# Gate fills three steps ahead of the value fills in place of two (induced-set attention and a gated feed-forward layer)

## The chip, the core and the metric

The kernel runs on one core of one Trainium2 chip. A core has TensorE (PE, matrix products, with its weight loads shown apart as PEld), VectorE (DVE), ScalarE (ACT), GpSimd (POOL) and SyncE (SP, which here only issues DMAs). Each engine takes its instructions in the order in which the program gives them. The metric is the device time of one execution in microseconds. Three runs of the kernel before took 770.77 us at the median (770.39 to 770.82).

## The reference

The input x has 4 batches of 12416 tokens of 128 numbers; there are 32 inducing points. Attention is done twice, then a gated feed-forward layer follows:

```
h   = softmax(scale * I @ x.T) @ x          # per batch: 32 x 128
y   = softmax(scale * x @ h.T) @ h          # per batch: 12416 x 128
out = (sigmoid(y @ w_gate) * (y @ w_val)) @ w_out
```

w_gate and w_val are 128 x 1536, w_out is 1536 x 128. All tokens of the four batches, 49664, go through the layer; the result is float32.

## The kernel before

Tokens lie as 128 partitions by 97 chunks for each batch. **Stage 1** makes the 32 attention rows h of a batch. **Stage 2** makes the 32 attention weights of every token, in groups of 16 chunks: scores on PE (line 361), the maximum on VectorE (372), two matmuls that subtract it (385), the exponential on ScalarE (394), the sum, the inverse and the normalised weights, four times side by side, on POOL (402 to 448). The result `a2n` is turned by a transposing DMA of SP's queue (459) into `a2r`, which has the 32 attention rows four times over, on partitions 0 to 31, 32 to 63 and so on.

The layer never forms y. Since y is a2 times h, y @ w_gate is a2 @ (h @ w_gate): for each batch `hw` holds h @ w_gate and h @ w_val, and a gate or value fill is a matmul with a contraction of 32 alone. Gates use the row groups 0 to 63 of the array and values the row groups 64 to 127, so that gate and value matmuls can run beside each other.

The main loop goes over **steps**. A block is 512 tokens (4 chunks); its 12 slices of 128 hidden columns are cut into steps of two slices and one slice in turn, so a block has 8 steps, and the 97 blocks have 776 (the last block takes the one odd chunk of each of the four batches). Even steps have two slices (two PSUM banks), odd steps one. A step t has

- a gate fill, `gate(t)`: one or two matmuls into a PSUM tile tagged g2 or g1, then a tanh of ScalarE (line 693) into `t16` (sigmoid is made from tanh, the halves are put in elsewhere);
- a value fill and product, `product(t)`: one or two matmuls into a PSUM tile tagged v2 or v1, then on VectorE (line 699) u = (t + 1) * v;
- a projection, `project`: for each slice four matmuls (line 715) that add u @ w_out to the tile `acc`. Behind the last slice of a block ScalarE copies `acc` out (line 727) and SP stores it (730).

PSUM is full: g2 and v2 take two banks each, g1, v1, `acc` and the tile "m" for all side work one each. Each tag has one buffer. So gate fills of even steps follow each other through one tile, and those of odd steps through another: a gate fill waits until the tanh of two steps earlier has read the same tile, and likewise a value fill until the product two steps earlier is done. The matmuls of gate and value fills are all recorded at line 678.

The order on every engine is written out by hand (`manual_schedule`): what the Python program emits first stands first in its engine's queue. The loop emits for each step the value fill and product, then a gate fill ahead, and then, behind even steps, `beside` (one slot of the side work: loads, stage 1 of the next batch, stage 2 of later groups), behind odd steps `project` with mostly three slices. Stage 1's side work puts a maximum on VectorE (189), an exponential on ScalarE (202) and, later, sums on PE (235) and a copy on ScalarE (245).

## Time and profile before

| what | value |
|---|---|
| median of three runs | 770.77 us |
| the profiled execution | 771.34 us |
| its span | 769.6 us |
| TensorE's granted clock, mean | 0.984 |
| VectorE busy | 735.9 us (96%) |
| ScalarE busy | 672.6 us (87%) |
| TensorE busy | 671.3 us (87%) |
| GpSimd busy | 279.8 us (36%) |
| products, line 699 | 776, 692.0 us |
| tanh, line 693 | 776, 598.6 us |
| projection matmuls, line 715 | 4656, 329.8 us |

The span is the time from the first to the last instruction of the profiled execution; what lies around it (1.7 us here) is in the execution's time alone. A group's line has the instructions' count, then their busy time and the mean of one in ns, then the idle time of the engine just before them and what ended most of it. In a timeline a line has the start, the length, the engine and line, the operation, and in brackets the idle time before it with its releaser. Records of one kind that follow each other are merged into one line. In a row of windows, the stretch comes first, then its length, the busy time of PE, PEld, DVE, ACT and POOL with their instructions, and then PE's granted clock, the DMA share and GB/s.

### The profile page before, as it was taken

The numbers are of one execution on the slowest core, as the hardware profiler recorded it, in microseconds if no ns is written. First come the engines' busy times: TensorE is split into PE (matmuls) and PEld (weight loads), VectorE is DVE, ScalarE is ACT, GpSimd is POOL, SyncE is SP. The second block draws the span as 40 slices with busy tenths as digits, with TensorE's granted clock in tenths as the row PEclk, the third lists the DMA queues.
The fourth block names the chain that finished last, engine by engine and source line by source line (L and its number), as shares of the span: only waits on it lengthen the run. The fifth ranks groups of instructions, "written<-read, shape, count | busy, mean of one in ns | idle before, by whom it ended". The sixth has DMA issues, their size and how long they took to land.

```text
span 769.6 us, 20801 instructions
## 1 busy us (share of the span) xinstructions
PE 671.3 (87%) x8167; PEld 403.5 (52%) x8167; DVE 735.9 (96%) x908; ACT 672.6 (87%) x1007; POOL 279.8 (36%) x445
## 2 busy tenths in 40 slices
PE   6788889899888898989888889988988888988887
PEld 4354555555555455555555455555555555555554
DVE  3798999999999999999999999999999999999997
ACT  4687989889989999989989899988989899899996
POOL 3551450472440523545504224246235135045100
PEclk9688999999999999999999999999999999999999
DMA  8979735424239255174056632121121220230311
GB/s 167 152 129 189 139 62 107 98 55 99 71 83 165 66 109 122 36 117 99 29 97 133 117 84 63 49 57 51 49 70 35 64 69 31 69 69 29 72 43 43
DMA packets 117730, 65.16 MB, mean 85 GB/s; under 512 B 101344, under 2 KB 102016, under 8 KB 117632
## 3 DMA queue, kind: packets, MB, share of 16 engines
q1 hardware_dynamic: 112192, 49.94, 28.2%
q0 software_dynamic: 5440, 13.90, 11.5%
q8 instruction: 64, 1.05, 0.6%
q14 instruction: 34, 0.28, 0.1%
HBM read 27.80 MB, written 25.43 MB: 69 GB/s over the span
## 4 chain that ended last, share of the span: by engine, by line
DVE 37%; PE 25%; issue 20%; ACT 13%; DMA 2%; POOL 2%; ACTq 0%; DVEq 0%; POOLq 0%
DVE u L699 33%; PE acc_ps L715 10%; PE v_ps L678 10%; ACT t L693 10%; PE s_ps L361 2%; DMA a2r<-a2n 2%; DVE nmx L372 2%; PE g_ps L678 1%; ACT e L394 1%; DVE nm L189 1%; ACT a1T L202 1%; PE xt_ps L493 1%; DMA xn<-in_x_dram 1%; PE s_ps L385 0%; POOL a2n L448 0%
## 5 line engine op out<-in xcount | busy, mean ns | idle before, releaser
L699 DVE SCALAR_TENSOR_TENSOR u<-t,v_ps 128x1024 f16<-128x1024 f16 (+1 forms) x776 | 692.0, 948 | 12.8 <-PE g_ps L678 4.7
L693 ACT ACTIVATE t<-g_ps 128x1024 f16<-128x1024 f32 (+1 forms) x776 | 598.6, 819 | 69.7 <-PE g_ps L678 53.9
L678 PE MATMUL v_ps<-a2r,hwt 32*128 32x512 f16 (+1 forms) x1188 | 293.8, 372 | 77.8 <-DVE u L699 73.6
L715 PE MATMUL acc_ps<-wo,u 128*128 128x128 f16 x4656 | 329.8, 221 | 0.9
L715 PEld LDWEIGHTS <-u 128*128 128x128 f16 x4656 | 263.7, 98 | 98.6 <-issue 97.1
L678 PE MATMUL g_ps<-a2r,hwt 32*128 32x512 f16 (+1 forms) x1188 | 296.6, 379 | 1.9 <-DMA a2r<-a2n 1.2
L678 PEld LDWEIGHTS <-hwt 32*128 32x128 f16 x2400 | 99.8, 91 | 214.2 <-issue 166.2
L376 POOL CAST hi<-nmx 128x16 bf16<-128x16 f32 (+2 forms) x28 | 5.5, 195 | 279.6 <-DVE nmx L372 279.5
L448 POOL TENSOR_TENSOR a2n<-e,rs 128x2048 f16<-128x2048 f16 (+2 forms) x28 | 86.9, 3105 | 5.0 <-PE g_ps L678 2.9
L426 POOL TENSOR_TENSOR near<-sme,minus 128x16 f32<-128x16 f32 (+1 forms) x27 | 69.7, 2583 | 2.1
L727 ACT ACTIVATE o<-acc_ps 128x512 f32<-128x512 f32 x97 | 58.8, 607 | 4.6 <-PE acc_ps L715 4.6
L402 POOL TENSOR_TENSOR sum<-e 128x256 f32<-128x256 f16 (+1 forms) x27 | 16.1, 598 | 88.2 <-ACT e L394 88.2
L402 POOL TENSOR_TENSOR sum<-sum 128x128 f32<-128x128 f32 (+3 forms) x108 | 31.5, 292 | 8.5
L361 PEld LDWEIGHTS <-xT 128*128 128x128 f16 x388 | 13.7, 97 | 12.8 <-issue 12.5
L361 PE MATMUL s_ps<-hT,xT 128*128 128x32 f16 x388 | 18.2, 179 | 0.9 <-DVE hT L287 0.5
L372 DVE TENSOR_REDUCE nmx<-s_ps 128x16 f32<-128x512 f32 (+2 forms) x28 | 17.0, 606 | 0.8 <-PE s_ps L361 0.8
L202 ACT ACTIVATE a1T<-s_ps,nm 128x512 f16<-128x512 f32 (+1 forms) x24 | 15.1, 630 | 1.7 <-DVE nm L189 1.7
L189 DVE TENSOR_REDUCE nm<-s_ps 128x1 f32<-128x512 f32 (+1 forms) x24 | 14.7, 614 | 0.9 <-PE s_ps L177 0.9
L82 POOL DMA_DIRECT2D xn<-in_x_dram x25 | 15.1, 612 | 0.9 <-POOLq L840 0.8
L394 ACT ACTIVATE e<-s_ps 128x512 f16<-128x512 f32 (+2 forms) x28 | 14.9, 533 | 0.6 <-PE s_ps L385 0.6
L497 ACT COPY xT<-xt_ps 128x1024 f16<-128x1024 f16 (+1 forms) x6 | 5.6, 939 | 8.5 <-PE xt_ps L493 8.5
L495 DVE COPY xT<-xt_ps 128x1024 f16<-128x1024 f16 (+2 forms) x8 | 4.7, 598 | 8.7 <-PE xt_ps L493 8.7
(104 smaller groups left out, 200.6 us busy)
## 6 DMA issues: line engine op xcount, KB each, us to landing
out_dram<-o SPq DMA_DIRECT2D x97, 256.0 KB, 2.4
xn<-in_x_dram POOLq DMA_DIRECT2D x19, 512.0 KB, 6.9
xn<-in_x_dram POOLq DMA_DIRECT2D x4, 544.0 KB, 6.0
a2r<-a2n SPq DMA_TRANSPOSE x29, 4.9
xn<-in_x_dram POOLq DMA_DIRECT2D x1, 384.0 KB, 14.3
wg<-in_moe_w_gate_dram POOLq DMA_DIRECT2D x1, 384.0 KB, 4.5
wv<-in_moe_w_val_dram POOLq DMA_DIRECT2D x1, 384.0 KB, 6.4
wo<-in_moe_w_out_dram POOLq DMA_DIRECT2D x1, 384.0 KB, 6.6
```

The costliest lines, as they stand in the source:

```text
L202: nc.scalar.activation(out=a1T[0:R, 0 : w * P], in_=s1[0:R, 0 : w * P], func=AF.Exp, bias=nm[0:R, col], accum_out=l1[0:R, col],)
L361: nc.tensor.matmul(s2[:, j, :], xT[b][:, c + j, :], hT16[b][:], start=(j == 0), stop=whole and j == j1 - 1, skip_group_check=True,)
L372: nc.vector.tensor_reduce(out=nmx[:, 0:n], in_=s2[:, 0:n, :], axis=AX.X, op=ALU.max, negate=True)
L394: nc.scalar.activation(out=e[:, 0:n, :], in_=s2[:, 0:n, :], func=AF.Exp, scale=SCALE)
L402: nc.gpsimd.tensor_tensor(out=d[:, 0:n, :], in0=src[:, :, 0:w], in1=src[:, :, w : 2 * w], op=ALU.add)
L426: nc.gpsimd.tensor_tensor(out=near[:, 0:n], in0=sme[:, 0:n], in1=minus1[:, 0:n], op=ALU.pow)
L448: eng.tensor_tensor(out=a2n[:, 0:n, :, :], in0=e.unsqueeze(2).to_broadcast((P, n, 4, m)), in1=rs.unsqueeze(2).unsqueeze(3).to_broadcast((P ...
L678: nc.tensor.matmul(pt[:, k, col : col + nb * P], hw[b][r : r + 32, j // 2, :], a2r[r : r + 32, o : o + nb, :].rearrange("p j t -> p (j t)" ...
L693: nc.scalar.activation(out=st["t"][:], in_=st["g"][:], func=AF.Tanh, scale=0.5)
L699: nc.vector.scalar_tensor_tensor(out=st["u"][:], in0=st["t"][:], scalar=1.0, in1=st["v"][:], op0=ALU.add, op1=ALU.mult)
L715: nc.tensor.matmul(acc[0][:, i, :], st["u"][:, k, ts(i, P)], wo16[:, j, :], start=(j == 0 and i == 0), stop=(j == NJ - 1), skip_group_chec ...
L727: nc.scalar.mul(out=o32[:], in_=acc[0][:], mul=0.5)
```

## The change

The gate fill that follows the value fill of step t is that of step t+3 in place of step t+2. Ahead of the loop three gates are filled in place of two. Nothing else is edited: tiles, buffers, the side work and the projections are the same.

```diff
+AHEAD = 3
...
-    gate(0)
-    gate(1)
+    for t in range(AHEAD):
+        gate(t)
     for t in range(NST):
         product(t)
-        gate(t + 2)
+        gate(t + AHEAD)
         if t % 2 == 0:
             beside(t // 2)
         else:
```

A gate fill of step t+3 has the other parity than step t: beside the two-slice value fill of an even step now stands a one-slice gate fill, and beside the one-slice value fill of an odd step a two-slice gate fill.

## The prediction

> **What bounds the kernel now.** I read the page first: span, busy shares, chain, the two costliest groups.

> ```profile
> span 769.6 us, 20801 instructions
> PE 671.3 (87%) x8167; PEld 403.5 (52%) x8167; DVE 735.9 (96%) x908; ACT 672.6 (87%) x1007; POOL 279.8 (36%) x445
> DVE 37%; PE 25%; issue 20%; ACT 13%; DMA 2%; POOL 2%; ACTq 0%; DVEq 0%; POOLq 0%
> L699 DVE SCALAR_TENSOR_TENSOR u<-t,v_ps 128x1024 f16<-128x1024 f16 (+1 forms) x776 | 692.0, 948 | 12.8 <-PE g_ps L678 4.7
> L693 ACT ACTIVATE t<-g_ps 128x1024 f16<-128x1024 f32 (+1 forms) x776 | 598.6, 819 | 69.7 <-PE g_ps L678 53.9
> ```

> The reader is to see that VectorE is the bound: its 776 products take 692.0 of 769.6 us, and all idle time ahead of them is 12.8 us. ScalarE waits 53.9 us for gate fills, but it has that time to spare. Next, PE's timeline in an undisturbed stretch:

> ```profile
> 391.77 0.39 PE L678 MATMUL v_ps<-a2r,hwt 32*128 32x512 f16 x2
> 391.78 0.39 PE L678 MATMUL g_ps<-a2r,hwt 32*128 32x512 f16 x2
> 392.37 0.37 PE L678 MATMUL v_ps<-a2r,hwt 32*128 32x512 f16 x1 [0.20 <-DVE u L699]
> 392.69 0.84 PE L715 MATMUL acc_ps<-wo,u 128*128 128x128 f16 x12
> 393.55 0.39 PE L678 MATMUL v_ps<-a2r,hwt 32*128 32x512 f16 x2
> ```

> A pair of steps (two banks, then one) takes 393.55-391.77 = 1.78 us. The chain of waits has the two-bank product that follows the 391.77 fill start at 392.27, 0.50 after it; it ends 1.22 later, at 393.49, and 0.06 later the next two-bank value fill starts. 0.50 + 1.22 + 0.06 = 1.78: the pace is set by product and value fill taking turns on the one value buffer. No gate is in this ring. A gate can only hurt it, by making PE late: a value fill may be late by what the ring leaves. After the projection (0.84 for 12 matmuls, the next fill following 0.78 from its start where PE is behind, 0.86 here) that is 0.08.

> **The change, part by part.** No instruction is added or removed: every gate step still issues its one or two matmuls with weight loads and one tanh; it issues no DMA, so on SP nothing is passed. What moves is its place: one step earlier on PE, passing one value fill and, every second time, a projection or the side matmuls of `beside`; and one step earlier on ScalarE, passing the side work there (the output copy, exponentials). On POOL and VectorE it has nothing. The gate buffers stay two, so gate t+3 goes where gate t+1 was, and waits for tanh t+1 in place of tanh t. Behind a waiting gate PE's queue holds the projection or the next value fill.

> *Steady pairs.* I set 0 at the start of a two-bank product; then the fills are at -0.50 (two banks), 0.10 (one), the projection at 0.42, the next two-bank fill at 1.28. A tanh starts 0.46 after its gate (388.24 to 388.70), the two-bank one takes 1.02, the one-bank one 0.60, overlapping by about 0.1. Before: two-bank tanh -0.04 to 0.98, one-bank 0.88 to 1.47; the gate that waits for it is due at 1.88. After: one-bank -0.04 to 0.56, two-bank 0.56 to 1.58, due at 1.88. Neither waits: cost 0. The cover is 0.25 us (0.30 less 0.05 from end to release).

> ```profile
> 388.70 1.51 ACT L693 ACTIVATE t<-g_ps 128x1024 f16<-128x1024 f32 x2 [0.26 <-PE g_ps L678]
> 390.10 0.60 ACT L727 ACTIVATE o<-acc_ps 128x512 f32<-128x512 f32 x1
> ```

> *Output copy, 97 times.* Before: it runs from 390.10 to 390.70 and the next block's projection starts at 390.92, 0.22 later. After, it stands behind a two-bank tanh that starts 0.46 after the fill at 388.83, so it starts at 390.22 and ends at 390.82: cover 0.10, 0.05 of it release. Cost 0; the next tanh is 0.1 later, which is slack gone, no more.

> *Exponentials of stage 1 (21 times in the loop, 0.67 each from start to start).* These make a gate wait now:

> ```profile
> 272.49 0.37 PE L678 MATMUL v_ps<-a2r,hwt 32*128 32x512 f16 x1 [0.20 <-DVE u L699]
> 272.91 0.37 PE L678 MATMUL g_ps<-a2r,hwt 32*128 32x512 f16 x1
> 273.22 0.84 PE L715 MATMUL acc_ps<-wo,u 128*128 128x128 f16 x12
> ```

> The gate waits 0.42 behind the value fill, and the projection behind the gate. After, the sum on ScalarE is the same (one tanh of each kind and the exponential lie ahead of that gate in both orders): from -0.04, before 0.92+0.67+0.60, after 0.48+0.67+1.02, both 2.13 to 2.15 against 1.88. So 12 of the 21 cost what they cost now. Nine follow an output copy of the pair before (82.1 after 80.7, 271.6 after 270.2 and their like). There ScalarE comes in 0.1 later than before; by the steady pair a gate then waits 0.50 in place of 0.41, and by the rows about 270 us 0.17 more. I take 0.13 for eight (the ninth, at 62.9, lies ahead of the wait below): +1.0. Ends: 0 (exponentials start 0.25 to 0.4 earlier in that order, and a side matmul that waits for one, 0.13, is freed) and 9 x 0.3 = 2.7.

> *Start.*

> ```profile
> 33.57 1.51 ACT L693 ACTIVATE t<-g_ps 128x1024 f16<-128x1024 f32 x2 [1.45 <-PE v_ps L678]
> 34.62 1.22 DVE L699 SCALAR_TENSOR_TENSOR u<-t,v_ps 128x1024 f16<-128x1024 f16 x1
> 34.64 0.61 PE L678 MATMUL g_ps<-a2first,hwt 32*128 32x512 f16 x2 [0.71 <-ACT t L693]
> ```

> Gate 2 waits for tanh 0 till 34.64. Now value fill 0 is ahead of it; after, behind it. Product 0 then starts at 34.64+0.70 = 35.34, 0.72 later. Followed through gates 4 and 6 (each again waiting for a tanh, with fills behind), product 8, at 44.69 now, comes 0.3 to 0.85 later: I take +0.55.

> *First landing of attention weights (a2r).* One gate waits for a DMA:

> ```profile
> 64.26 0.37 PE L678 MATMUL g_ps<-a2r,hwt 32*128 32x512 f16 x1
> 64.56 0.84 PE L715 MATMUL acc_ps<-wo,u 128*128 128x128 f16 x12
> 65.34 0.39 PE L678 MATMUL v_ps<-a2r,hwt 32*128 32x512 f16 x2
> 66.92 0.49 PE L678 MATMUL g_ps<-a2r,hwt 32*128 32x512 f16 x2 [1.20 <-DMA a2r<-a2n]
> ```

> This gate, of step 32, moves ahead of the projection at 64.56 and the fill at 65.34. If the landing keeps its place, projection and fill follow it: fill at 66.92+0.30+1.39 = 68.6 (1.39 is the projection's length at the slow clock, 68.21 to 69.60), product at 69.3 in place of 65.82. Part comes back, since now VectorE waits 0.80 and 1.19 just behind, and more while the clock is low: product 32 at about 72 in place of 70.32, product 36 some 0.65 later than the 75.27 it has. All other landings are 5 us or more ahead of their gates (the next: 92.03 for a tanh at 100.92). I take +0.65; ends 0 (landing earlier) and 2.0 (another half-speed stretch).

> ```profile
> 67.10:73.90 6.80, 6.80 (x50) 3.26 (x48) 4.32 (x5) 4.86 (x7) 0.41 (x2) 0.50 1.01 212
> ```

> This row has PE's clock at 0.50 from 67.1 to 73.9, right after the wait of 1.20. With PE idle from 64.6 it could stay there for half as long again, 3.4 us, worth about 1.0; I leave that to the range. [...]

> *Sum.* 0 + 0 + 1.0 + 0.55 + 0.65 = +2.2 us. The profiled execution took 771.34 us, span 769.6 and 1.7 around it, 0.57 over the median of the runs. Its like would take 773.5; the median 770.77 + 2.2 = 773.0, 0.29% slower. About 0.2%, 1.5 us, is what a measurement of this kernel can tell from no change.

> **Rivals.** *Faster: the lead removes VectorE's waits for tanh.* VectorE's waits from 76 us on:

> ```profile
> DVE u L699 <- ACT t L693: 3.1, 14, 0.3
> DVE u L699 <- PE g_ps L678: 1.3, 4, 0.4
> ```

> Were all 18, and two like them of 0.3, late gates, 5.0 us would go: 770.8 - 5.0 + 1.2 (start and DMA) = 767.0. Against it: the product at 403.65 is put down to a tanh, but its own tanh (401.65, 1.02 long) was over a microsecond before, and its value fill started at 403.15, the usual 0.50 earlier. PE was late, through two side matmuls; the gates' lead does not move those. For it: the releasers' labels. It decides once more than 1.2 + 1.5 = 2.7 us of these waits vanish. Chance 0.14.

> *No difference:* start and DMA costs are swallowed by the waits that lie behind them now, and the exponentials cancel: 770 to 772.3, about 771.2. Chance 0.27.

> *Much slower: the output copy falls on the projection.* It has 0.05 of cover after release and 0.08 in the ring. Were it 0.2 later than I have it, some 70 blocks would lose 0.07 each: 773.0 + 4.9 = 777.9. It speaks for it that ten copies already end 0.05 ahead of the projection that follows. Chance 0.08.

> That the order is not taken over I count at nothing: it is written out by hand.

> **How the numbers follow.** My forecast (1.5 to 5 us slower) has 0.51. Faster by over 0.2%: 0.14. Within: 0.27. Slower: 0.51 + 0.08 = 0.59. Range: low end 770.0, taking in no difference; high end 776.0, where the upper ends (exponentials 2.7, DMA 2.0, start 0.85 over the median give 776.3) nearly meet. Left out are the faster case and most of the last, 0.2. The forecast's own range is 772.3 to 775.5.

> **What would show it.** The steady pair stays at 1.78, with the one-bank gate beside the two-bank fill. Product 0 starts near 35.3. The gate that waits for the DMA stands behind the one-bank fill and ahead of a projection, waiting about 2.5 us. Behind exponentials a two-bank gate waits 0.3 to 0.55, and VectorE's waits from 76 us on are not fewer than 20. I am wrong if VectorE's idle time from 76 us falls by microseconds (faster), if the pair's length moves by even 0.01 (388 pairs make 4 us of it), or if projections wait for output copies (slower).

## The result, and the profile after

The kernel with three gates ahead took 778.96 us (median of six runs, 777.22 to 780.06) beside 770.18 us for the kernel before (six runs, 768.26 to 770.82): a ratio of 1.0117, with a 95% interval of 1.0102 to 1.0132. It is slower by 8.8 us where 2.2 had been forecast, and lies above the range. The side was right, the size was not.

The profiled execution took 780.06 us. The page after, with its span, busy shares and the two costliest groups:

```profile
span 778.2 us, 20825 instructions
PE 680.6 (87%) x8167; PEld 409.6 (53%) x8167; DVE 736.7 (95%) x908; ACT 689.0 (89%) x1007; POOL 279.9 (36%) x445
...
L700 DVE SCALAR_TENSOR_TENSOR u<-t,v_ps 128x1024 f16<-128x1024 f16 (+1 forms) x776 | 692.9, 950 | 22.3 <-ACT t L694 9.1
L694 ACT ACTIVATE t<-g_ps 128x1024 f16<-128x1024 f32 (+1 forms) x776 | 614.2, 816 | 61.3 <-PE g_ps L679 48.5
```

The products take what they took (692.9 against 692.0 us). VectorE's idle time ahead of them is 22.3 in place of 12.8: VectorE waits more, it doesn't work more. Its waits from 76 us on, with the time in total, the count and the longest:

```profile
DVE u L700 <- ACT t L694: 5.4, 15, 0.4
DVE u L700 <- ACT o L728: 3.0, 4, 1.0
DVE u L700 <- PE g_ps L679: 2.6, 6, 1.0
DVE u L700 <- issue: 0.8, 2, 0.4
DVE u L700 <- PE hp_ps L236: 0.3, 1, 0.3
```

That is 28 waits of 12.1 us, where there were 20 of 5.0. They aren't spread over the loop. Three of the four put down to the output copy `o` (0.98, 0.92 and 0.73) stand at 160.34, 344.27 and 528.20, where PE's clock is at 0.50; PE's own waits from 76 us on hold no projection that waits for a copy. An undisturbed pair is as it was, in PE's timeline of the kernel after:

```profile
398.43 0.39 PE L679 MATMUL v_ps<-a2r,hwt 32*128 32x512 f16 x2
398.43 0.39 PE L679 MATMUL g_ps<-a2r,hwt 32*128 32x512 f16 x1
399.02 0.37 PE L679 MATMUL v_ps<-a2r,hwt 32*128 32x512 f16 x1 [0.20 <-DVE u L700]
399.03 0.39 PE L679 MATMUL g_ps<-a2r,hwt 32*128 32x512 f16 x2
399.35 0.84 PE L716 MATMUL acc_ps<-wo,u 128*128 128x128 f16 x12
400.20 0.39 PE L679 MATMUL v_ps<-a2r,hwt 32*128 32x512 f16 x2
```

400.20 - 398.43 = 1.77 us for a pair, and the one-slice gate stands beside the two-slice value fill. (The 1.78 of the prediction is the same length, rounded: over the 24 pairs of steps 64 to 112 the two kernels drift apart by 0.02 us in all.) To find where the time went, I set each product's start against the same product's start in the kernel before. The difference at the last product is 8.6 us. It grows like this (half clock stands for a granted clock of 0.50):

| steps | what lies there | growth, us |
|---|---|---|
| 0 to 36 | start, first landing of `a2r` | -0.27 |
| 36 to 56 | two jumps of 0.18 | +0.37 |
| 56 to 64 | a stretch of PE at half clock, 99.4 to 102.8 us | +1.45 |
| 112 to 128 | combine of batch 1 | +2.10 |
| 128 to 304 | four jumps of 0.14 to 0.18 | +0.71 |
| 304 to 320 | combine of batch 2 | +2.24 |
| 320 to 496 | four jumps of 0.14 to 0.18 | +0.76 |
| 496 to 512 | combine of batch 3 | +1.24 |

The three combines are 5.58 of the 8.6 us. `combine` (line 302 on) is the piece of side work that joins a batch's partial sums: POOL gathers the minima in `quad`, VectorE reduces them in four short instructions (0.72 us in all) to `col`, ScalarE takes the exponential of seven columns, `w`, from `col`, and POOL weights the sums with it. The prediction doesn't mention it. In the kernel before, ScalarE's timeline and then PE's show it so:

```profile
153.12 0.30 ACT L321 ACTIVATE w<-nm,col 128x7 f32<-128x7 f32 x1 [0.90 <-DVE col L314]
153.33 1.98 ACT L693 ACTIVATE t<-g_ps 128x512 f16<-128x512 f32 x3
...
153.86 0.37 PE L678 MATMUL v_ps<-a2r,hwt 32*128 32x512 f16 x1 [0.96 <-DVE u L699]
153.96 0.37 PE L678 MATMUL g_ps<-a2r,hwt 32*128 32x512 f16 x1
```

And in the kernel after, ScalarE's, PE's and VectorE's timelines:

```profile
154.69 0.30 ACT L322 ACTIVATE w<-nm,col 128x7 f32<-128x7 f32 x1 [1.33 <-DVE col L315]
154.90 3.21 ACT L694 ACTIVATE t<-g_ps 128x1024 f16<-128x1024 f32 x4
...
155.43 0.37 PE L679 MATMUL v_ps<-a2r,hwt 32*128 32x512 f16 x1 [0.96 <-DVE u L700]
155.95 0.39 PE L679 MATMUL g_ps<-a2r,hwt 32*128 32x512 f16 x2 [0.15 <-ACT t L694]
156.28 0.51 PE L716 MATMUL acc_ps<-wo,u 128*128 128x128 f16 x6
...
157.54 1.22 DVE L700 SCALAR_TENSOR_TENSOR u<-t,v_ps 128x1024 f16<-128x1024 f16 x1 [0.43 <-ACT t L694]
```

In both, ScalarE stands still until VectorE has the minima. Its tanh in the queue behind `w` must run before PE may fill the next gate. Before, the first tanh behind `w` is a one-slice tanh (0.58 of the merged 1.98), and the one-slice gate follows the value fill by 0.10 us. After, it is a two-slice tanh (154.90 to 155.90), the two-slice gate follows its value fill by 0.52, and the projection and VectorE's next product stand behind that gate. So the wait costs about 0.4 us more by itself. That is a fifth of what the segment loses. The rest is in the windows around it (stretch, length, then busy time and instructions of PE, PEld, DVE, ACT, POOL, then PE's granted clock, the DMA share and GB/s), first of the kernel after, then of the kernel before:

```profile
154.01:157.42 3.41, 2.29 (x25) 1.16 (x23) 3.02 (x8) 2.67 (x4) 1.94 (x6) 1.00 0.00 1
157.42:160.83 3.41, 3.41 (x40) 2.04 (x37) 2.31 (x3) 2.76 (x5) 3.17 (x5) 0.50 0.00 0
160.83:164.25 3.42, 3.42 (x30) 2.27 (x28) 3.04 (x4) 2.24 (x4) 0.83 (x3) 0.50 0.83 165
```

```profile
152.41:155.82 3.41, 2.44 (x34) 1.40 (x32) 3.34 (x9) 2.43 (x5) 1.91 (x6) 1.00 0.00 2
155.82:159.23 3.41, 3.13 (x44) 1.99 (x43) 3.41 (x5) 3.36 (x6) 3.17 (x5) 1.00 0.21 77
```

After, PE's clock is at 0.50 for 6.8 us behind the combine, and VectorE, whose idle time is lost time here, is busy for 2.31 and 3.04 of 3.41 us. Before, it stays at 1.00. The other two combines have 6.8 and 3.4 us at half clock after, and none before.

### The profile page after: what moved, and what is told of

Its sections match the earlier page's. It is cut to its first block, busy times and chain, and to the rows that moved or that the text cites. A ratio compares the mean times of both kernels' runs of the same rounds, so it can differ in the third digit from the quotient of the medians.

```text
span 778.2 us, 20825 instructions
## 1 busy us (share of the span) xinstructions
PE 680.6 (87%) x8167; PEld 409.6 (53%) x8167; DVE 736.7 (95%) x908; ACT 689.0 (89%) x1007; POOL 279.9 (36%) x445
## 4 chain that ended last, share of the span: by engine, by line
DVE 36%; PE 28%; issue 21%; ACT 8%; DMA 4%; POOL 2%; DVEq 0%; ACTq 0%; POOLq 0%
DVE u L700 33%; PE acc_ps L716 12%; PE v_ps L679 11%; ACT t L694 7%; DMA xn<-in_x_dram 2%; PE s_ps L362 2%; DMA a2r<-a2n 2%; PE g_ps L679 2%; PE s_ps L386 2%; DVE nm L190 1%; ACT o L728 1%; ACT a1T L203 1%; DVE nmx L373 1%; POOL a2n L449 0%; POOL xn L83 0%
## 5 line engine op out<-in xcount | busy, mean ns | idle before, releaser
L700 DVE SCALAR_TENSOR_TENSOR u<-t,v_ps 128x1024 f16<-128x1024 f16 (+1 forms) x776 | 692.9, 950 | 22.3 <-ACT t L694 9.1
L694 ACT ACTIVATE t<-g_ps 128x1024 f16<-128x1024 f32 (+1 forms) x776 | 614.2, 816 | 61.3 <-PE g_ps L679 48.5
L716 PE MATMUL acc_ps<-wo,u 128*128 128x128 f16 x4656 | 334.9, 223 | 1.0
L716 PEld LDWEIGHTS <-u 128*128 128x128 f16 x4656 | 268.5, 99 | 91.3 <-issue 89.6
L679 PE MATMUL g_ps<-a2r,hwt 32*128 32x512 f16 (+1 forms) x1188 | 301.0, 383 | 4.6 <-DMA a2r<-a2n 2.2
L679 PEld LDWEIGHTS <-hwt 32*128 32x128 f16 x2400 | 102.5, 91 | 223.9 <-issue 174.8
```

Source lines behind the costliest of these rows:

```text
L679: nc.tensor.matmul(pt[:, k, col : col + nb * P], hw[b][r : r + 32, j // 2, :], a2r[r : r + 32, o : o + nb, :].rearrange("p j t -> p (j t)" ...
L694: nc.scalar.activation(out=st["t"][:], in_=st["g"][:], func=AF.Tanh, scale=0.5)
L700: nc.vector.scalar_tensor_tensor(out=st["u"][:], in0=st["t"][:], scalar=1.0, in1=st["v"][:], op0=ALU.add, op1=ALU.mult)
L716: nc.tensor.matmul(acc[0][:, i, :], st["u"][:, k, ts(i, P)], wo16[:, j, :], start=(j == 0 and i == 0), stop=(j == NJ - 1), skip_group_chec ...
```

## The experiments

My theory was: (1) the place of the two-slice tanh behind `w` delays a gate by some 0.4 us at each combine, and (2) PE's pause there makes its clock fall, which costs more than the wait. (The share of about 0.7 that the expectations set for PE lies between the windows above: 2.29 of 3.41 us after is 0.67, with the clock at 0.50 behind it, 2.44 before is 0.72, with 1.00.) The rivals were that the half-clock stretches come by chance from the loop as a whole (B in the expectations); that the wait costs and the clock nothing (C); a general loss (the output copies on the projections, as in the prediction's last rival); and a loss from the start and the first landing that the chance of the clock hides in this profile. Growths in the three combine segments are given as above, against the same profile of the kernel before (the kernel after has 2.10, 2.24 and 1.24).

**w a slot later, in both kernels.** If `w` is emitted one slot of `beside` later, ScalarE shouldn't wait for the minima at all. The edit was made to the kernel after and, as a control, to the kernel before:

```diff
                 op=ALU.min,
             )
+        yield
         w1 = bp.tile([P, NS], F32, tag="w1")
```

> The changed kernel, with the weight exponential of the combine (w1) emitted one slot later, so that VectorE's minima are done when ScalarE comes to it. Theory A (combine): in each of the three combines ScalarE stands still for VectorE, a two-bank tanh follows, PE's gate waits 0.5 us for it, PE's busy share of that 3.4 us falls below about 0.7 and its clock is halved; together about 2 us three times. Then this takes about 773.3 (772 to 775) where the changed kernel took 779.0, and no half-speed stretch lies within 10 us behind a combine. Rival B (the half-speed stretches come from the loop as a whole, by chance of where the 3.4 us fall): 777.5 or more. Rival C (the wait alone costs, the clock nothing): about 777.7.

> The kernel before, with the same edit, as a control. Theory A: its gate waits only 0.10 us there and no product is late, so it stays within 1 us of the kernel before (770.2). If the edit itself saves time whatever the order of the gates, this is 3 us or more below 770.

Measured: 781.91 us (779.78 to 784.30; ratio 1.0164, 1.0142 to 1.0185) from the kernel after, and from the kernel before 776.53 (median of eleven, 768.54 to 782.56; the eight below 779 have a ratio of 1.0059, 1.0033 to 1.0086). Both expectations fell, and the control shows that the edit is to blame. The extra slot keeps the combine's multiplications off POOL's queue for longer, so that the next load of x no longer stands behind them. POOL's timeline, first of the control, then of the kernel before:

```profile
143.80 0.53 POOL L82 DMA_DIRECT2D xn<-in_x_dram  x1
```

```profile
159.07 0.62 POOL L82 DMA_DIRECT2D xn<-in_x_dram  x1
```

The load is issued 15 us earlier and runs beside the transposing DMA that makes `a2r`, which SyncE issues from 142.42 on in the control. A gate then waits for that, for 3.00 us in the control and 2.26 in the edited kernel after. PE's timeline of the control:

```profile
163.36 0.61 PE L679 MATMUL g_ps<-a2r,hwt 32*128 32x512 f16 x2 [3.00 <-DMA a2r<-a2n]
```

At the first combine the segments lost 4.04 us (from the kernel after) and 5.05 (the control) to this. At the second they lost 1.26, with 3.4 us at half clock, and 0.91, where a gate waits 0.56 for such a DMA again. At the third, where no such load lies near, both have -0.04: there the wait is gone and so is all the loss. That is a hint for the theory, but the time of this pair says nothing about it.

**A slower w in the kernel before.** A copy on ScalarE behind `w` (nobody uses its result) holds the one-slice tanh back by about as much as the order does after:

```diff
         nc.scalar.activation(out=w1[:], in_=nm1[:], func=AF.Exp, bias=col[:], scale=-1.0)
+        junk = bp.tile([P, 3, C], F32, tag="junk")
+        nc.scalar.copy(out=junk[:], in_=hst[:, 0:3, :])
```

> The kernel before, with one more ScalarE copy of 128x384 numbers (about 0.4 us from start to start) behind the combine's exponential: the suspected wait alone, in the old order. Theory A: the gate's wait grows from 0.10 to about 0.5, products are 0.35 late three times and the clock is halved behind at least two of the three combines: 774 to 776.5. Rival C (the wait alone): 771.2. Rival B: 770 to 771, with no new half-speed stretch.

Measured: 773.86 us (771.56 to 774.70), ratio 1.0054 (1.0039 to 1.0069); the segments have +2.18, +0.42 and +1.16. PE's timeline at the second combine:

```profile
333.57 0.37 PE L680 MATMUL v_ps<-a2r,hwt 32*128 32x512 f16 x1 [0.96 <-DVE u L701]
334.08 0.37 PE L680 MATMUL g_ps<-a2r,hwt 32*128 32x512 f16 x1
```

The gate follows its value fill by 0.51, as after the change, with two gates ahead as before. This combine loses 0.42, and no stretch at half clock follows it. The other two lose 2.18 and 1.16, and behind them the clock is at 0.50 for 6.8 and 3.4 us. So the wait suffices without the change, it costs 0.42 alone, and the rest comes with the clock and not every time. The median lies just below what the theory gave (774), and one combine of three kept its clock in the profile. That profile is of the shortest of the six runs: no gate waits for the first landing in it, so it is 3.7 us ahead of the kernel before when the first combine comes, and its own time of 771.56 doesn't show the 3.76 us of the combines.

**PE kept busy in the pause.** In the kernel after, three matmuls of 512 columns whose result nobody reads fill PE's wait at each combine; ScalarE's wait is left as it is:

```diff
         add_tree(hx, NS)
-        for _ in range(COMBINE_LAG):
+        yield "take"
+        idle = ps.tile([P, 512], F32, tag="m", name="idle_ps")
+        for k in range(3):
+            nc.tensor.matmul(
+                idle[:], ident[:], wo16[:, 4 * k : 4 * k + 4, :], start=True, stop=True
+            )
+        yield "give"
+        for _ in range(COMBINE_LAG - 1):
             yield
```

> The changed kernel, with three idle matmuls of 512 columns (0.64 us) in the slot in which PE waits behind the combine's minima; their result is not used. Theory A: the gate still waits 0.5 us and a product is 0.4 late three times, but PE's busy share stays above 0.7 and the clock is not halved there: 4 us less than the changed kernel, about 775 (773.5 to 776). Rival C: no change, 779 or a little more. Rival B: 778 to 780.

Measured: 774.67 us (772.11 to 776.79), ratio 1.0065 (1.0045 to 1.0085). PE's timeline, and the windows there:

```profile
153.29 0.82 PE L337 MATMUL idle_ps<-wo,ident 128*128 128x512 f16 x3
154.32 0.37 PE L686 MATMUL v_ps<-a2r,hwt 32*128 32x512 f16 x1 [0.21 <-DVE u L707]
154.84 0.39 PE L686 MATMUL g_ps<-a2r,hwt 32*128 32x512 f16 x2 [0.15 <-ACT t L701]
```

```profile
152.86:156.27 3.41, 3.04 (x27) 1.43 (x25) 3.06 (x8) 2.64 (x4) 1.90 (x6) 1.00 0.00 0
156.27:159.68 3.41, 3.41 (x55) 2.34 (x53) 3.25 (x4) 3.27 (x6) 3.17 (x5) 1.00 0.06 23
```

The gate still waits 0.52, PE is busy for 3.04 in place of 2.29 us of the window, and the clock stays at 1.00, at all three combines. Each loses 0.45, 0.45 and 0.44. More work on PE made the kernel 4.3 us faster: the longest of its six runs (776.79) is below the shortest of the kernel after (777.22), and rivals B and C had both given 778 or more. This is the run that splits the 5.58 us of the combines: 1.34 are the wait, 4.24 the clock in this profile. The segments between the combines keep their +0.71 and +0.77, so those are something else. No output copy was touched, so the rival that puts the loss on copies falls.

**The minima a slot earlier, in both kernels.** VectorE's minima come one slot earlier and `w` stays in its slot, so POOL's queue keeps its order:

```diff
-        for _ in range(COMBINE_LAG):
+        for _ in range(COMBINE_LAG - 1):
             yield
         col = bp.tile([P, 1], F32, tag="col")
...
             )
+        yield
         w1 = bp.tile([P, NS], F32, tag="w1")
```

> The changed kernel, with the combine's minima on VectorE emitted one slot earlier and the weight exponential and all that follows it in their old slots, so that ScalarE finds the minima done and nothing moves on GpSimd's queue. Theory A (ScalarE held for the minima, and the clock halved behind it): about 773.3 (772 to 775) where the changed kernel took 779.0; the gate behind the combine waits under 0.2 us and no half-speed stretch follows a combine. Rival B (half-speed stretches come by chance): 777.5 or more.

> The kernel before with the combine's minima one slot earlier: the control for the same edit in the changed kernel. Theory A: nothing to save here (the gate waits 0.10 us and no product is late), so 769 to 771. If the edit saves time in any order, under 768.5.

Measured, from the kernel after: 773.21 us (770.96 to 775.23), ratio 1.0051 (1.0031 to 1.0072), 5.75 below the kernel after. The control, from the kernel before: 770.98 (768.98 to 773.02), ratio 1.0019 (1.0002 to 1.0037), segments of -0.05 each. So the edit gains nothing by itself with two gates ahead. With three ahead, ScalarE's and PE's timelines:

```profile
151.82 0.29 ACT L323 ACTIVATE w<-nm,col 128x7 f32<-128x7 f32 x1
...
152.22 0.37 PE L680 MATMUL v_ps<-a2r,hwt 32*128 32x512 f16 x1 [0.96 <-DVE u L701]
152.23 0.39 PE L680 MATMUL g_ps<-a2r,hwt 32*128 32x512 f16 x2
```

`w` waits for nothing and the gate stands right behind its value fill. One part of the expectation missed: behind two of three combines the clock still fell for 3.4 us (segments +1.01, +1.17, -0.05). VectorE's minima alone leave PE with a wait of 0.96, and at two of the three the clock fell behind it.

**The start undone, or the start alone.** The lead is switched at step 36, behind the first landing. Two gates ahead first, then three; three first, then two; and two first, then three, together with the earlier minima:

```diff
-    for t in range(AHEAD):
-        gate(t)
-    for t in range(NST):
-        product(t)
-        gate(t + AHEAD)
+    filled = 0
+    for t in range(-1, NST):
+        if t >= 0:
+            product(t)
+        while filled <= t + (2 if t < 36 else 3):
+            gate(filled)
+            filled += 1
+        if t < 0:
+            continue
```

> Two gates ahead up to step 35, three from there on: the start and the wait for the first landing as before, the rest as changed. Theory: the changed kernel less what the start and that wait cost it, 0.6 to 1.6 us: 777.4 to 778.4. If the start were the larger part of the loss: under 775.

> Three gates ahead up to step 35, two from there on: the start and the wait for the first landing alone. Theory: 0.6 to 1.6 us over the kernel before (769.8), 770.4 to 771.4, the gate of step 32 waiting about 2.3 us ahead of a projection. If the start were the larger part of the loss: over 774.

> The changed kernel with both edits: the minima one slot earlier, and two gates ahead up to step 35. What is left by the theory are the exponentials behind output copies, eight times 0.15, and a half-speed stretch about 99 us in some runs: 771 to 773. If something else in the steady loop costs, 775 or more.

Measured: two then three 780.21 us (778.43 to 780.82; ratio 1.0139, 1.0120 to 1.0158), three then two 771.32 (768.41 to 774.60; 1.0025, 1.0008 to 1.0043), two then three with the earlier minima 773.53 (769.32 to 774.86; 1.0048, 1.0028 to 1.0068). The first missed. Undoing the start gains nothing, because the switch itself costs 0.9 us (steps 36 to 40) and because the combines are 2.54, 2.54 and 2.53 here, each with 6.8 us at half clock. Three then two came as expected, and flat: the combines have 0.01 at most. With the lead of three at the start alone, the loop loses nothing after 104 us. The landing looks as the prediction had it, in PE's timeline:

```profile
63.93 0.39 PE L679 MATMUL v_ps<-a2r,hwt 32*128 32x512 f16 x1
67.05 0.61 PE L679 MATMUL g_ps<-a2r,hwt 32*128 32x512 f16 x2 [2.73 <-DMA a2r<-a2n]
```

Its profile has +0.97 by step 48, and +1.45 from a half-clock stretch at 100.6 us. There the lead is two, so that stretch, which the kernel after also has, isn't tied to the lead of three at its place. The third, with the earlier minima, has combines of -0.05, -0.04 and -0.05; it lies half a microsecond above what was expected and is level with the earlier minima alone (773.21). What the start and the landing cost can't be told from the chance of the clock in this pair; three then two puts it at 771.32 - 769.86 = 1.5 us, its interval from 0.6 to 3.3.

**Stage 1 a slot later.** The jumps of 0.14 to 0.18 between the combines lie where an exponential of stage 1 (at one jump of each four, one of stage 2) comes one pair behind an output copy. PE's timeline after, at such a place:

```profile
276.69 0.37 PE L679 MATMUL v_ps<-a2r,hwt 32*128 32x512 f16 x1 [0.21 <-DVE u L700]
277.26 0.39 PE L679 MATMUL g_ps<-a2r,hwt 32*128 32x512 f16 x2 [0.21 <-ACT t L694]
```

The gate waits 0.57 behind the value fill; before, 0.42. To test that the output copy matters and not the exponential alone, stage 1 was moved by one slot in both kernels:

```diff
-                work.append((at + 5 + 6 * g, 2, lambda b=b, g=g: stage1(b + 1, g)))
+                work.append((at + 6 + 6 * g, 2, lambda b=b, g=g: stage1(b + 1, g)))
```

> The changed kernel with stage 1 of the next batch one slot later, so that its exponentials no longer stand one pair behind an output copy but in the same pair or two behind. Against the kernel before with the same shift, products between steps 128 and 304 lose 0.15 us once or not at all, where the changed kernel loses 0.7 in four steps of 0.14 to 0.18. If every exponential costs, whatever its place, the 0.7 stays.

> The kernel before with the same shift, as the reference for the run ahead of this one; its own time is of no matter, as the shift may move transfers too.

Measured, one time each: 774.14 and 771.24 us. Between the combines the shifted kernel after drifts against the shifted kernel before by 0.03 us (steps 128 to 304) and 0.05 (320 to 496), in place of 0.71 and 0.76. So an exponential costs the lead of three something only behind an output copy. The combines of the shifted kernel after have 0.45, 0.46 and 2.20: two kept their clock, with the wait as it was and no filler on PE, and one lost it.

**Loads later in the kernel before.** The prediction's landing wait is there before the change, too. Two loads of batch 1's x (those of groups 4 and 5) are moved seven slots later, away from the transposing DMA of the first `a2r`; the lead is two:

```diff
-                    loads.append((at + 5 * g - 12, "x", 1, g))
+                    loads.append((at + 5 * g - (12 if g == 3 else 5), "x", 1, g))
```

> The kernel before, with two loads of the next batch's x (groups 4 and 5) seven slots later, so that they do not share the DMA engines with the first turned attention weights. If the late landing at 66.9 us comes from those loads, it lands before 62 us, no gate waits for it, the clock is not halved behind it, and the time is about 767 (766 to 768.5) against 769.9. If not, no change.

Measured: 767.70 us (767.07 to 768.47, twelve runs), ratio 0.9971 (0.9958 to 0.9984): faster than both kernels. PE's timeline, and a window:

```profile
63.96 0.39 PE L678 MATMUL v_ps<-a2r,hwt 32*128 32x512 f16 x1
64.16 0.37 PE L678 MATMUL g_ps<-a2r,hwt 32*128 32x512 f16 x1
```

```profile
67.07:73.90 6.83, 6.03 (x82) 3.22 (x81) 6.68 (x9) 6.21 (x11) 2.42 (x8) 1.00 1.13 191
```

No gate waits for the DMA, and the stretch that had the clock at 0.50 in the kernel before has 1.00. The profile is 3.5 us ahead by step 48 and stays there. The landing itself came at 63.1 (66.9 in the kernel before), a little later than expected (before 62). Of the two loads one is issued at 53.83 all the same, as POOL's queue held it until 53.95 in the kernel before; only the other left the DMA's neighbourhood, from 54.61 to 74.12.

## Why the prediction was right or wrong

- **Steady pair: right.** 1.77 us, no wait, no cost. None of the prediction's three signs of being wrong came: VectorE's idle time did not fall, the pair kept its length, and no projection waited for an output copy. It had no sign for a large loss of another kind.
- **Output copy: right, cost nothing.** The copy of 396.85 to 397.44 ends 0.14 ahead of its projection, where 0.10 was worked out. The prediction's slowest case, 777.9, came near the measured number by a mechanism that isn't there.
- **Exponentials: mechanism right, size low.** It took eight at 0.13, or 1.0. There are ten jumps of 0.14 to 0.18, 1.68 in sum: the eight, and two exponentials of stage 2 that also come behind an output copy, which it hadn't counted. The other twelve of the 21 cost what they did: no jump stands at them.
- **Start: right at its first step.** Product 0 comes 2.48 us after the first gate in place of 1.70: +0.78, where 0.72 was given. By product 8 only 0.06 of it is left in this profile, as the clock rose at 41.4 and not at 43.2 us.
- **First landing: right in its order.** The gate of step 32 waits 2.25 us behind the one-slice fill with projection and fill behind it ("about 2.5"). Start and landing together were put at 1.2; 1.5 was measured with the lead of three up to step 36 alone, with a wide interval.
- **The failed step: the list of side work that the gate's tanh passes on ScalarE.** The prediction wrote "one step earlier on ScalarE, passing the side work there (the output copy, exponentials)", and then costed output copies and stage 1's exponentials. Left out was the exponential of the combine, which differs from all others in that ScalarE stands still in front of it for VectorE. The page had it, in the view of the waits of ScalarE in the kernel before, with the time in total, the count and the longest:

```profile
ACT w L321 <- DVE col L314: 2.7, 3, 0.9
```

  The prediction gives these three waits no price and no reason for that; it speaks of the 53.9 us for gate fills alone. They cost 3 x 0.45 = 1.3 us when the order behind them changes.
- **The second failed step: the clock, looked at in one place alone.** The prediction saw half clock after a wait of 1.20 and left another 3.4 us of it, "worth about 1.0", to the range, at the landing. The combines' PE waits of 0.96 and then 0.15, inside a window with PE busy for 2.29 us, do the same three times: 4.2 us. One more stretch, at 99 us, adds 1.45.

With these two, the terms of the profile are 1.68 (exponentials), 1.34 (combine waits), 4.24 (clock behind the combines) and 1.45 (clock at 99 us): 8.7. Start and landing are -0.27 in this profile, which makes 8.4 of the 8.6 found; the other 0.2 are drifts of a few hundredths between the jumps. Of the prediction's own terms the exponentials made 1.68 of this loss, and start and landing none of it; the rest comes from terms that it hadn't priced, so the right side says little for the sum. (Its forecast of 1.5 to 5 us slower ends at 775.8, not at the 775.5 given.) All but the term at 99 us were tied to their cause by a run: the combines by a slower `w`, filled PE and earlier minima, the exponentials by the shift. Why the clock falls at one combine and not at the next, the last section reads from the traces.

## What to carry to other kernels

When a queue runs one step further ahead, go through every instruction of that engine which itself waits for another engine, however few they are: what stands behind its release changes, and a short job there may become a long one. Price a wait of PE not by its length alone but by the matmuls that are left in the 3.41 us that it falls in, since a gate's wait of half a microsecond cost from 0.42 to 2.54 us at a combine here. And look at all queues after moving one instruction: a single slot let a load of x out 15 us earlier and cost more than what was to be measured, which only the control showed.

## What was unexpected of the hardware

```profile
95.98:99.39 3.41, 2.30 (x32) 1.37 (x30) 3.09 (x6) 2.95 (x5) 0.41 (x2) 1.00 0.71 107
```

```profile
150.94:154.35 3.41, 2.25 (x28) 1.40 (x28) 3.34 (x8) 2.75 (x6) 0.49 (x3) 1.00 0.58 187
```

```profile
97.79:101.20 3.41, 2.27 (x24) 1.13 (x24) 3.41 (x6) 2.21 (x4) 0.41 (x2) 1.00 0.22 71
```

What separates them here is how much work the matmuls in them do. Count a matmul by its columns times the share of 128 rows (and of 128 columns of weights) that its form in the profile gives, 32*128 for a fill and 128*128 for a projection, in units of one projection matmul: 128 columns through all rows are 1, a fill matmul of 512 columns through 32 rows is 1 as well, a filler of 512 columns through all rows is 4. Spread each from its start over 0.216 us for 512 columns, the distance of the fillers' starts, or twice that at half clock (the projection's matmuls start 0.056 us apart at full clock and 0.107 at half in the kernel before), and cut it at the window's borders:

| window of the grid | PE busy, us | count | clock in the next |
|---|---|---|---|
| after, 95.98 | 2.30 | 23.0 | 0.50 |
| after, first combine, 154.01 | 2.29 | 21.3 | 0.50 |
| before, first combine, 152.41 | 2.44 | 25.4 | 1.00 |
| before, 97.79 | 2.27 | 29.7 | 1.00 |
| both edits, 150.94 | 2.25 | 27.3 | 1.00 |
| slower `w`, first combine, 149.15 | 2.31 | 21.3 | 0.50 |
| slower `w`, second combine, 330.06 | 2.34 | 25.9 | 1.00 |
| PE filled, 152.86 | 3.04 | 33.1 | 1.00 |

In the profiles before and after, from 44 us on, 413 windows are at full clock. Behind the six that count 15.5 to 23.0 the clock fell; behind the other 407, which count 25.4 or more, it didn't. Of ten windows at half clock, the four with 19.5 to 24.0 were followed by half clock again, the six with 25.5 to 27.9 by full clock. The windows of the other runs in the table fit. An undisturbed pair of 18 such matmuls in 1.77 us makes about 35 in a window. The count was found in these traces afterwards, and the fillers are the only run that raised it on purpose; but it leaves no window of these two profiles unexplained, the three combines of each included. What I take for chance is where the grid lies. Moving the window over the profiles that kept their clock gives, as an estimate from these traces with 24.2 as the limit (midway between 23.0 and 25.4), the share of the grid's positions at which the clock falls at a combine: 0.19 with two gates ahead, 0.70 with three (the fillers' profile, the fillers left out of the count), 0.3 with the minima earlier in either order, and none with the fillers in. The limit matters: with 23.0 or 25.4 the 0.19 would be 0.09 or 0.34.

What a fall cost here, in a loop in which VectorE and not PE sets the pace: 0.7 to 1.5 us for 3.4 us at half clock (1.16 - 0.42 at a combine of the slower `w`, 1.45 at 99 us after), 1.7 to 2.1 for 6.8 (2.10 - 0.45 at the first combine after, 2.54 - 0.45 with two then three).
